# Outputs' loads and divisors moved to GpSimd, and the gated unit's first half put in source order on four engines

## The chip, the cores and the metric

The kernel runs on one core of a Trainium2 chip. The metric is the device time of one execution in microseconds (us). The kernel before takes 2924.66 us, the median of three runs (2924.26 to 2926.47). The engines are named as in the profile: PE is TensorE, DVE VectorE, ACT ScalarE, POOL GpSimd and SP SyncE; PEld is PE's weight load, and SPq, POOLq are the DMA-issuing sides of SP and POOL.

## The reference

One transformer layer whose two norms are modulated by a conditioning vector, with S = 2048 rows, D = 576, 32 heads of 18, and F = 4608, all in float32:

```
mod = silu(c) @ w_mod                      # six vectors of 576: sa, ca, ga, sb, cb, gb
h = layernorm(x) * (1 + ca) + sa
q, k, v = split(h @ wqkv)                  # 32 heads of 18
o = softmax(q @ k.T / sqrt(18)) @ v
x = x + ga * (o @ wo)
h = layernorm(x) * (1 + cb) + sb
x = x + gb * ((sigmoid(h @ w_gate) * (h @ w_up)) @ w_down)
```

## The kernel before

Every product is done in split form: an operand is cast to a high part (F32R), the difference to the original is the low part, and high x high, high x low and low x high are added.

The layer runs in three stages. Norm, q, k and v take the time up to about 237 us. Attention follows, to about 1580 us: 32 units (two heads and one half of the query rows each) of 16 steps; each step's PE work is written out by hand as a string of letters (`EASY`, `FULL`), and PE keeps that order (`manual_schedule`), while the other engines' instructions are put in order by the scheduler. Beside it run generators that advance by one `yield` at each letter "w", which is every second step, about 5 us. `taken` stores a unit's outputs (`od`) and sums of the softmax (`sd`). `divisors` loads the sums, takes the reciprocal, stores it (`rd`) and broadcasts it over each head's 18 rows into `rx`. `load_o` loads 128 rows' outputs, divisors and residual, and `project_o` multiplies them on POOL and projects them on PE (L667). Rows 0 to 7 (`first_rows`) go all the way to the operands of the gated unit; of rows 8 to 15 only the first heads are projected during attention (`last_rows_project`).

The gated unit follows. It has two halves of the rows; each half runs over 18 blocks of 256 columns of F, and each block has seven products in place of eight, in the order `ORDER = (1, 6, 2, 7, 5, 4, 3)`, with 14 matmuls each (`product`, L1029). After product 6 and product 7 stands one half of the previous block's product with w_down (`down`, L1052 to L1073: 48 matmuls in eight groups, three PSUM buffers `d`, and on DVE one add into `Oa` a group, L1069). In the first half the operands of the weights are made as well: `prepare(n + LOOK)` makes those of the product three places ahead. POOL makes sums of the raw weights (S, L884), ACT casts (w, L918), DVE takes the difference for the most of it and POOL for the rest (w, L923), and SP stores the result for the second half (ws, L924). What a product leaves is added on DVE from PSUM (u2 L1211, u3 L1222 and L1227, p1 L1234, u2 L1239), and `gate` (L1032 to L1045) follows: sigmoid on ACT, multiplication on DVE, cast hh on ACT, difference hl on DVE. The PSUM name `x` has three buffers in turn, so the add that reads the third step's product frees the buffer in which the next block's product 1 puts its second half.

Through the first half, `last_rows` (L1111 to L1185) advances by one `yield` at every second product: the divisors and projection of the last heads (80 matmuls, L1146), the layer norm of four rows at a time (statistics L153, scales L164 to L174, normalized rows L683, with `z` loaded back from `x1d` at L1163), its transposes and copies (ev, L1154), and the operands for the second half (ho, L714, with differences on POOL, L716, L721 and L725). From `n == ORDERED`, the 56th product (block 8), PE is held to source order; before that, and on all other engines throughout, the scheduler sets the order.

Of the kernel before, what the change touches and what calls it, by code (L numbers as in the profile page):

```python
# [15 lines left out]
F32 = mybir.dt.float32  # L16
# [7 lines left out]
P = 128  # L24
# [24 lines left out]
FULL = "vtmmttmvtm", "tmttwmtmm"  # L49
ORDERED = 56  # L50


@with_exitstack
def tile_block(ctx, tc, x_in, wqkv, wo, w_gate, w_up, w_down, c_in, w_mod, out):
# [181 lines left out]
    x1p = dram.tile([P, 8, D], F32, name="x1p")  # L236
    od = dram.tile([2, D, HW], F32, name="od")
    sd = dram.tile([2, H, HW], F32, name="sd")
    rd = dram.tile([2, H, HW], F32, name="rd")
    rx = dram.tile([2, D, HW], F32, name="rx")  # L240
    wod = dram.tile([P, 2, 2, D], F32R, name="wod")
# [383 lines left out]
    def load_o(t):  # L625

        half, a = divmod(t, 8)
        cols = slice(a * P, (a + 1) * P)
        n = 4 if half == 0 else DL // P
        got = state["rows", t % 2]  # L630
        for i, src in enumerate((od, rx)):
            nc.sync.dma_start(
                got[:, i, 0 : n * P].rearrange("p (k q) -> p k q", q=P),
                src[half, 0 : n * P, cols].rearrange("(k p) q -> p k q", p=P),
            )
            if half == 0:
                for p0 in (0, 64):
                    nc.sync.dma_start(got[p0 : p0 + 64, i, DM:640], src[half, DM:D, cols])
        nc.sync.dma_start(got[:, 2, 0:D], x_rows[:, t, :])

    def project_o(t):
# [3 lines left out]
        width = 640 if t < 8 else DL  # L645
        o, r, xt = got[:, 0, 0:width], got[:, 1, 0:width], got[:, 2, 0:D]
        T = temp([P, 2048], F32R)
# [95 lines left out]
    def first_rows():  # L743
        yield from load_wo()
        whole = big.tile([P, 8, 640], F32, name="big")
        for i in range(2):
            state["rows", i] = whole[:, 3 * i : 3 * i + 3, :]
        state["spare"] = whole[:, 6, :]
        yield from divisors(0, 0, H, state["spare"])
# [361 lines left out]
    def last_rows():  # L1111
# [5 lines left out]
        with tc.tile_pool(name="fin", bufs=1, side="right") as pool:  # L1117
            w = pool.tile([P, 2, 2, D], F32R, name="w")
            nc.gpsimd.dma_start(w, wod)
            yield from divisors(1, DL // DH + 1, H, pool.tile([P, 256], F32, name="sums"))  # L1120
            for t0 in (0, 4):
                cols = slice(t0 * P, (t0 + 4) * P)
                o, r = (pool.tile([P, 2, 512], F32, name=n) for n in ("o", "r"))
                for to, src in ((o, od), (r, rx)):
                    nc.sync.dma_start(to[:, 0, :], src[1, DL:DM, cols])
                    for p0 in (0, 64):
                        nc.sync.dma_start(to[p0 : p0 + 64, 1, :], src[1, DM:D, cols])
                yield
                nc.vector.tensor_mul(o, o, r)
                hi = pool.tile([P, 2, 512], F32R, name="hi")  # L1130
                nc.scalar.copy(hi, o)
                oh, om = hi[:, 0, :], hi[:, 1, :]
                ol = pool.tile([P, 512], F32R, name="ol")
# [3 lines left out]
                for j in range(4):  # L1137
                    rows = slice(j * P, (j + 1) * P)
                    xt = pool.tile([P, D], F32, name="xt", bufs=2)
                    nc.sync.dma_start(xt, x1p[:, t0 + j, :])  # L1140
                    for h in range(2):
# [3 lines left out]
                        for n, (a, i, k) in enumerate(ts_):  # L1145
                            nc.tensor.matmul(  # L1146
                                acc[:, :HALF], a[:, rows], w[:, i, k, cols], start=n == 0, stop=n == 4
                            )
                        nc.vector.tensor_add(xt[:, cols], xt[:, cols], acc[:, :HALF])
                    nc.sync.dma_start(x1d[:, t0 + j, :], xt)  # L1150
                    yield

        def modulated(ev, pt, scale, bias):
# [126 lines left out]
```

## Time and profile before

| | us |
|---|---|
| median of three runs | 2924.66 |
| the profiled execution, its time | 2923.8 |
| its span, first to last instruction | 2922.0 |
| gated unit, first half: blocks 0 to 17 | 1580.0 to 2273.3 |
| gated unit, second half, from | 2273.3 |
| PE busy | 2837.4 |
| DVE busy | 2127.2 |
| ACT busy | 1599.7 |
| POOL busy | 796.2 |

A row of the page's groups has line, engine and operation, out<-in with shapes, count, busy time, mean ns of one, and behind the bar the idle time of the engine just before them with what ended it. A row of waits has the engine and line, what it waited for, and then total, times and longest. A row of the timeline has start, length, engine, line and operation, with the idle time before it in brackets. The granted clock of PE is 1.00 at full speed.

### The profile page before, as it was taken

How to read it: one execution, taken by the hardware profiler on the slowest of the kernel's cores; microseconds unless marked ns; L12 is line 12 of the kernel's file. 1: busy time of each engine (PE TensorE's matmuls, PEld its weight loads, DVE VectorE, ACT ScalarE, POOL GpSimd, SP SyncE). 2: the span in 40 equal slices, each digit the busy share in tenths (PEclk: the TensorE clock that was granted, in tenths of full speed). 3: DMA queues.
4: the chain of work that ended last, by engine and by line, in shares of the span. 5: the costliest groups of instructions: out<-in, count | busy, mean ns of one | idle time of the engine just before them, and what ended most of it. 6: DMA issues, size and time to landing. Idle time of an engine off the chain costs nothing.

```text
span 2922.0 us, 46657 instructions
## 1 busy us (share of the span) xinstructions
PE 2837.4 (97%) x16933; PEld 1875.6 (64%) x16933; DVE 2127.2 (73%) x3865; ACT 1599.7 (55%) x2993; POOL 796.2 (27%) x894
## 2 busy tenths in 40 slices
PE   7999999999999999999999899998999999999999
PEld 5874444444444443443444788887888888888888
DVE  7567889999998888998771678765777555555555
ACT  3227999999998888899786323432333111111111
POOL 3102024444122101660222434456743100000000
PEclk9999999999999999999999999999999999999999
DMA  5344124433224211322326676776666844444443
GB/s 173 115 149 145 63 80 142 142 134 130 76 67 133 75 40 49 103 81 68 119 85 217 224 263 229 238 257 231 219 209 234 303 171 168 168 168 168 159 159 137
DMA packets 158204, 444.83 MB, mean 152 GB/s; under 512 B 19347, under 2 KB 71831, under 8 KB 145687
## 3 DMA queue, kind: packets, MB, share of 16 engines
q1 hardware_dynamic: 143495, 366.03, 37.5%
q0 software_dynamic: 14480, 75.84, 7.2%
q8 instruction: 133, 2.18, 0.3%
q14 instruction: 96, 0.79, 0.1%
HBM read 278.87 MB, written 167.12 MB: 153 GB/s over the span
## 4 chain that ended last, share of the span: by engine, by line
PE 87%; DMA 4%; DVE 3%; POOL 2%; issue 2%; ACT 1%; SPq 1%; POOLq 0%; ACTq 0%; DVEq 0%
PE o L543 17%; PE d L1065 14%; PE x L1029 13%; PE s L961 13%; PE s L451 11%; PE bg L1029 5%; PE bu L1029 5%; PE s L299 4%; PE s L339 2%; PE s L667 2%; DMA q<-qd 1%; DVE w L923 1%; ACT p L965 1%; DMA ws<-w 1%; POOL S L884 1%
## 5 line engine op out<-in xcount | busy, mean ns | idle before, releaser
L965 ACT ACTIVATE p<-s 128x512 f32<-128x512 f32 x2048 | 1063.4, 611 | 145.3 <-PE s L961 86.6
L464 DVE TENSOR_REDUCE mx<-s 128x1 f32<-128x512 f32 x1568 | 1010.7, 684 | 135.7 <-PE s L451 97.8
L451 PE MATMUL s<-k,q 54*128 54x512 f32 x1920 | 613.6, 443 | 3.9 <-DVE mx L464 2.3
L961 PE MATMUL s<-q,k 56*128 56x512 f32 x1920 | 594.0, 431 | 6.4 <-DMA q<-mrows 4.9
L543 PE MATMUL o<-p,vaug 128*32 128x512 f32 x4096 | 557.0, 610 | 1.0 <-ACT oT L558 1.0
L961 PEld LDWEIGHTS s<-q,k 56*128 56x128 f32 x1920 | 301.0, 187 | 321.1 <-ACT p L965 163.6
L1065 PE MATMUL d<-wd,hh 128*128 128x288 f32 x2304 | 471.4, 299 | 24.3 <-DVE Oa L1069 23.6
L451 PEld LDWEIGHTS s<-k,q 54*128 54x128 f32 x1920 | 290.3, 185 | 235.1 <-ACT p L965 105.7
L1065 PEld LDWEIGHTS d<-wd,hh 128*128 128x128 f32 x2304 | 379.7, 191 | 35.9 <-DVE Oa L1069 29.1
L1069 DVE TENSOR_TENSOR Oa<-Oa,d 128x288 f32<-128x288 f32 x576 | 257.3, 452 | 154.7 <-PE d L1065 151.5
L1065 PE MATMUL d<-wd,hl 128*128 128x288 f32 x1152 | 344.4, 299 | 0.9 <-DVE hl L1045 0.9
L1029 PE MATMUL x<-k,w 128*128 128x512 f32 x994 | 239.0, 391 | 3.7 <-DVE u L1239 2.6
L1041 ACT ACTIVATE u<-u 128x512 f32<-128x512 f32 x72 | 45.5, 632 | 328.4 <-DVE u L1227 306.6
L1065 PEld LDWEIGHTS d<-wd,hl 128*128 128x128 f32 x1152 | 220.2, 191 | 1.1 <-DVE hl L1045 1.1
L1029 PEld LDWEIGHTS x<-k,w 128*128 128x128 f32 x994 | 184.4, 188 | 41.7 <-DVE u L1239 3.5
L543 PEld LDWEIGHTS o<-p,vaug 128*32 128x32 f32 x4096 | 83.5, 109 | 165.4 <-issue 147.5
L1038 ACT ACTIVATE sg<-x 128x512 f32<-128x512 f32 x36 | 21.5, 598 | 292.4 <-PE x L1029 292.4
L1071 POOL DMA_DIRECT2D out_dram<-Oa x16 | 8.7, 542 | 606.6 <-DVE Oa L1069 606.6
L459 DVE CUSTOM_DVE_ANT_0 rise<-s,rise 128x512 f32<-128x512 f32 x240 | 163.3, 681 | 0.3 <-PE s L961 0.2
L457 ACT ACTIVATE rise<-s 128x512 f32<-128x512 f32 x240 | 147.8, 616 | 0.7 <-PE s L451 0.6
L923 POOL TENSOR_TENSOR w<-S,w 64x256 fp32r<-64x256 f32 x69 | 70.1, 1016 | 219.6 <-ACT w L918 208.3
L1029 PE MATMUL x<-w,w 128*128 128x512 f32 x504 | 122.1, 391 | 1.3 <-ACT w L918 1.0
(215 smaller groups left out, 3681.5 us busy)
## 6 DMA issues: line engine op xcount, KB each, us to landing
w<-ws SPq DMA_DIRECT2D x126, 640.0 KB
ws<-w SPq DMA_DIRECT2D x124, 640.0 KB
wd<-wds SPq DMA_DIRECT2D x36, 1152.0 KB
wds<-w POOLq DMA_DIRECT2D x18, 1152.0 KB, 4.6
k<-kd SPq DMA_DIRECT2D x30, 360.0 KB
w<-in_B_w_down_dram POOLq DMA_DIRECT2D x18, 576.0 KB, 4.3
q<-qd SPq DMA_DIRECT2D x64, 144.0 KB
raw<-in_B_w_gate_dram SPq DMA_DIRECT2D x34, 256.0 KB
```

What stands on the lines that cost most here:

```text
L299: nc.tensor.matmul(acc, w, hT[:, t, cols], start=n == 0, stop=n == len(ts_) - 1)
L451: nc.tensor.matmul(sp, qs[rows, qt * P : (qt + 1) * P], ks[rows, kc * 512 : (kc + 1) * 512], start=True, stop=True,)
L457: nc.scalar.activation(rise, sp, AF.Relu)
L459: nc.vector.tensor_tensor_reduce(rise, sp, rise, 1.0, -3.0e38, ALU.add, ALU.max, mx[0][:, qt, 0:1])
L464: nc.vector.tensor_reduce(mx[h][:, qt, j : j + 1], sp, axis=AX.X, op=ALU.max)
L543: nc.tensor.matmul(acc[32 * j : 32 * j + 32, :], vaug[:, kt, (2 * p + h) * VW : (2 * p + h) * VW + 32], probs[2 * c + h], start=kt == 0, s ...
L923: eng.tensor_sub(w[rows, :, to, :], src[rows, :, a, :], w[rows, :, a, :].bitcast(F32))
L961: nc.tensor.matmul(sT, ks[rows, kcols], qs[rows, c * 512 : (c + 1) * 512], start=True, stop=True)
L965: state["exp"] = nc.scalar.activation(pr, sT, AF.Exp, scale=SCALE)
L1029: nc.tensor.matmul(acc[v], w[:, v, a, :], X[s][:, b, :], start=first and n == 0, stop=n == 6, skip_group_check=not first,)
L1065: nc.tensor.matmul(acc[:, :HALF], a[:, f, rows], w[:, f, cols], start=n == 0, stop=n == 5)
L1069: nc.vector.tensor_add(Oa[:, t, cols], Oa[:, t, cols], acc[:, :HALF])
```

## The change

The diff has three parts. In the stores and loads of attention's outputs, `od` and `rx` become one tensor `orx`, a unit's four sums are stored by one DMA instead of four, and the loads of `load_o` and the three DMAs of `divisors` are issued by GpSimd instead of SyncE; the store of the reciprocals has a `yield` of its own between it and the reciprocal, and the residual rows have three tiles of their own. In `last_rows` the loads and stores go to GpSimd as well, a turn ahead or a turn later, and the multiplication, the copy and the differences are apart by `yield`s. In the main loop, PE, ACT, DVE and POOL are held to source order from product 0 to the end of the first half, and PE alone after it, where before PE alone was from product 56.

```
@@ taken
-            nc.sync.dma_start(od[half, f0 : f0 + DH, cols], oT[32 * j : 32 * j + DH, :])
-            nc.sync.dma_start(sd[half, 2 * p + h : 2 * p + h + 1, cols], oT[32 * j + DH : 32 * j + VW, :])
+            nc.sync.dma_start(orx[0, half, f0 : f0 + DH, cols], oT[32 * j : 32 * j + DH, :])
+        nc.sync.dma_start(
+            sd[half, 2 * p : 2 * p + 2, :].rearrange("h (c q) -> (h c) q", c=2), oT[DH:P:32, :]
+        )
@@ divisors
-        nc.sync.dma_start(t, flat(sd))
+        nc.gpsimd.dma_start(t, flat(sd))
         yield
         nc.vector.reciprocal(t, t)
-        nc.sync.dma_start(flat(rd), t)
-        yield
-        nc.sync.dma_start(
-            rx[half, h0 * DH : h1 * DH, :].rearrange("(h e) q -> h e q", e=DH),
+        yield
+        nc.gpsimd.dma_start(flat(rd), t)
+        yield
+        nc.gpsimd.dma_start(
+            orx[1, half, h0 * DH : h1 * DH, :].rearrange("(h e) q -> h e q", e=DH),
@@ load_o
-        got = state["rows", t % 2]
-        for i, src in enumerate((od, rx)):
-            nc.sync.dma_start(
+        got, xt = state["rows", t % 2], state["x", t % 3]
+        for i in range(2):
+            nc.gpsimd.dma_start(
                 got[:, i, 0 : n * P].rearrange("p (k q) -> p k q", q=P),
-                src[half, 0 : n * P, cols].rearrange("(k p) q -> p k q", p=P),
+                orx[i, half, 0 : n * P, cols].rearrange("(k p) q -> p k q", p=P),
             )
...
-        nc.sync.dma_start(got[:, 2, 0:D], x_rows[:, t, :])
+        nc.gpsimd.dma_start(xt, x_rows[:, t, :])
@@ last_rows
+            def load_heads_end(t0):
+                both = pool.tile([P, 2, 2, 512], F32, name="both")
...
+            def load_rows(j):
+                xt = pool.tile([P, D], F32, name="xt", bufs=3)
+                nc.gpsimd.dma_start(xt, x1p[:, j, :])
+                return xt
...
                 for j in range(4):
-                    nc.sync.dma_start(xt, x1p[:, t0 + j, :])
+                    if j < 3:
+                        rows.append(load_rows(t0 + j + 1))
+                    if j == 0 and t0 == 0:
+                        both = load_heads_end(4)
+                    if done:
+                        nc.gpsimd.dma_start(*done)
...
-                    nc.sync.dma_start(x1d[:, t0 + j, :], xt)
+                    done = x1d[:, t0 + j, :], xt
                     yield
@@ main loop
-        if n == ORDERED:
+        if n == 0:
+            manual.enter_context(tc.manual_schedule(engines={
+                mybir.EngineType.PE, mybir.EngineType.Activation, mybir.EngineType.DVE, mybir.EngineType.Pool,
+            }))
+        if n == 7 * NB:
+            manual.close()
             manual.enter_context(tc.manual_schedule(engines={mybir.EngineType.PE}))
```

Three places of the order, before and after. In the rows, the first number is the place on its engine, then the line, the operation, and the tiles; line numbers after the change are three higher for most of the gated unit.

DVE in the tail of a block of the first half, before; `u` is u3 at L1227 and u2 at L1239, `w` the low part of a weight:

```order
2648 L1227 TENSOR_TENSOR u_23237<-x,u_23237 128x512 x2
2649 L1042 TENSOR_TENSOR u_23237<-u_23237 128x512
2650 L923 TENSOR_TENSOR w<-S_23343,w 128x2x256
2651 L1234 TENSOR_TENSOR p_23089<-bg,p_23089 128x512
2652 L1045 TENSOR_TENSOR hl_23210<-u_23237,hh_23209 128x512
2653 L1234 TENSOR_TENSOR p_23089<-bu,p_23089 128x512
2654 L1042 TENSOR_TENSOR p_23089<-p_23089 128x512
2655 L923 TENSOR_TENSOR w<-raw_23068,w 128x2x256
2656 L1239 TENSOR_TENSOR u_23113<-x,u_23113 128x512
```

The same place after:

```order
2640 L926 TENSOR_TENSOR w<-raw_23201,w 128x2x256
2641 L1258 TENSOR_TENSOR u_23444<-x,u_23444 128x512 x2
2642 L1045 TENSOR_TENSOR u_23444<-u_23444 128x512
2643 L1048 TENSOR_TENSOR hl_23409<-u_23444,hh_23408 128x512
2644 L926 TENSOR_TENSOR w<-S_23550,w 128x2x256
2645 L1265 TENSOR_TENSOR p_23288<-bg,p_23288 128x512
2646 L1265 TENSOR_TENSOR p_23288<-bu,p_23288 128x512
2647 L1045 TENSOR_TENSOR p_23288<-p_23288 128x512
2648 L1048 TENSOR_TENSOR hl_23407<-p_23288,hh_23406 128x512
2649 L926 TENSOR_TENSOR w<-raw_23267,w 128x2x256
2650 L1270 TENSOR_TENSOR u_23320<-x,u_23320 128x512 x2
```

Each step's w has moved from behind the multiplication and between the next step's adds to ahead of the adds, and hl from among the next step's adds to the end of its own step.

DVE at the layer norm of four of the last rows, behind product 6, before; BN_STATS and BN_AGGR are the statistics, `z` the rows, `Oa` the adds of the down product:

```order
2674 L1069 TENSOR_TENSOR Oa<-Oa,d 128x288
2675 L154 BN_AGGR mv_2208<-st 128x2
2676 L1069 TENSOR_TENSOR Oa<-Oa,d 128x288
2677 L164 TENSOR_SCALAR var<-mv_2208 128x4
2678 L1069 TENSOR_TENSOR Oa<-Oa,d 128x288
2679 L923 TENSOR_TENSOR w<-raw_23068,w 128x2x256
2680 L1069 TENSOR_TENSOR Oa<-Oa,d 128x288 x2
2681 L169 RECIPROCAL r_23474<-sd 128x4
2682 L171 TENSOR_TENSOR sd<-r_23474 128x4
2683 L1069 TENSOR_TENSOR Oa<-Oa,d 128x288
2684 L172 TENSOR_TENSOR sd<-sd,var 128x4
```

The same place after:

```order
2662 L153 BN_AGGR mv_2207<-st 128x2
2663 L152 BN_STATS st<-z 128x6 x2
2664 L153 BN_AGGR mv_2207<-st 128x2
2665 L163 TENSOR_SCALAR var<-mv_2207 128x4
2666 L168 RECIPROCAL r_23705<-sd 128x4
2667 L170 TENSOR_TENSOR sd<-r_23705 128x4
2668 L171 TENSOR_TENSOR sd<-sd,var 128x4
2669 L172 TENSOR_SCALAR sd<-sd 128x4
2670 L173 TENSOR_TENSOR rs_2208<-r_23705,sd 128x4
2671 L684 TENSOR_SCALAR z<-z,mv_2207,rs_2208 128x2x288 x4
2672 L1072 TENSOR_TENSOR Oa<-Oa,d 128x288 x8
```

The adds into Oa, which stood among the norm's instructions, now all stand behind the last of them.

GpSimd in attention, after, at the divisors of the second half's first heads; these DMAs were on SyncE before:

```order
351 L631 DMA big<-orx 128x3x128 x2
352 L572 DMA big<-sd 88x256
353 L576 DMA rd<-big 88x256
354 L578 DMA orx<-rd 396x1x1024
355 L631 DMA big<-orx 128x3x128 x2
356 L650 TENSOR_TENSOR big<-big 128x384
```

All of them now stand in one queue, with the multiplication that needs the loads right behind them. The loads of `z` stay on SyncE; after, their place there is:

```order
604 L864 DMA raw_22801<-in_B_w_up_dram 128x1x256
605 L927 DMA ws<-w 128x1280 x2
606 L1189 DMA z<-x1d 128x288 x8
607 L927 DMA ws<-w 128x1280
608 L862 DMA raw_23267<-in_B_w_gate_dram 128x2x256
```

The eight loads stand behind two stores of weight pairs.

More of the change, by code (lines that the diff above doesn't have):

```diff
@@ L49 @@
 FULL = "vtmmttmvtm", "tmttwmtmm"
-ORDERED = 56
 @with_exitstack
@@ L746, in first_rows @@
         for i in range(2):
-            state["rows", i] = whole[:, 3 * i : 3 * i + 3, :]
-        state["spare"] = whole[:, 6, :]
+            state["rows", i] = whole[:, 2 * i : 2 * i + 2, :]
+        for i in range(3):
+            state["x", i] = whole[:, 4 + i, 0:D]
+        state["spare"] = whole[:, 7, :]
         yield from divisors(0, 0, H, state["spare"])
@@ L1146, in last_rows @@
                             nc.tensor.matmul(
-                                acc[:, :HALF], a[:, rows], w[:, i, k, cols], start=n == 0, stop=n == 4
+                                acc[:, :HALF], a[:, part], w[:, i, k, cols], start=n == 0, stop=n == 4
                             )
                         nc.vector.tensor_add(xt[:, cols], xt[:, cols], acc[:, :HALF])
-                    nc.sync.dma_start(x1d[:, t0 + j, :], xt)
+                    done = x1d[:, t0 + j, :], xt
                     yield
+            nc.gpsimd.dma_start(*done)
         def modulated(ev, pt, scale, bias):
```

40 lines of the change are left out of this document (24 added, 16 removed).

## The prediction

> **What bounds the kernel now.** I read the page first, then a table of windows cut at the gated unit's block borders, then PE's waits there, then the timelines of one undisturbed block.
>
> ```profile
> span 2922.0 us, 46657 instructions
> PE 2837.4 (97%) x16933; PEld 1875.6 (64%) x16933; DVE 2127.2 (73%) x3865; ACT 1599.7 (55%) x2993; POOL 796.2 (27%) x894
> ```
>
> TensorE (PE) is busy for 97% of the span, so the work itself stays and only PE's waits, and the half clock behind a long wait, can go or come. They are found by block. In the rows below (stretch, its length, then PE, PEld, DVE, ACT, POOL busy with counts, and PE's granted clock) each stretch is one block of the first half, from block 0; the row of 693.30 is the whole half.
>
> ```profile
> 1580.00:1605.40 25.40, 23.09 (x99) 18.14 (x98) 11.66 (x17) 10.26 (x15) 9.57 (x10) 1.00 0.80 269
> 1605.40:1647.40 42.00, 38.43 (x195) 32.17 (x196) 33.18 (x47) 13.69 (x21) 26.30 (x24) 0.96 0.79 269
> 1647.40:1696.30 48.90, 43.12 (x225) 37.31 (x224) 31.10 (x51) 13.12 (x20) 14.86 (x16) 0.93 0.54 181
> ...
> 1776.20:1814.50 38.30, 36.57 (x207) 32.13 (x206) 32.07 (x64) 15.49 (x22) 18.17 (x19) 1.00 0.73 242
> 1814.50:1851.20 36.70, 36.70 (x209) 32.44 (x208) 26.37 (x41) 14.06 (x21) 16.98 (x15) 1.00 0.67 232
> ...
> 1925.70:1966.90 41.20, 37.27 (x195) 32.39 (x194) 27.55 (x42) 15.10 (x24) 30.52 (x26) 0.96 0.80 277
> ...
> 2055.10:2098.40 43.30, 37.77 (x195) 33.31 (x194) 30.36 (x44) 13.86 (x22) 31.71 (x28) 0.92 0.62 218
> ...
> 2168.30:2203.30 35.00, 35.00 (x195) 31.12 (x195) 25.68 (x42) 11.42 (x18) 16.88 (x16) 1.00 0.62 211
> ...
> 1580.00:2273.30 693.30, 654.55 (x3525) 573.11 (x3525) 489.91 (x784) 232.23 (x346) 347.27 (x317) 0.98 0.70 238
> ```
>
> Block 15 (from 2168.30) has no wait: 35.0 us. Were all like it, the half would take 23.1 (PE's work in block 0) + 17 x 35.0 = 618.1 us. It takes 693.3, so 75.2 us are excess: 9.3 in blocks 0 and 1, 13.9 in block 2, 32.7 in blocks 9 to 12 (1925.7 to 2098.4 is 172.7, less 140.0), the other 19.3 in the blocks between. This 75.2 is all that a better order can win; PE's waits of this stretch, and ACT's idle time ahead of its copies of the last rows' operands, say who ends them:
>
> ```profile
> PE d L1065 <- DVE Oa L1069: 23.6, 12, 4.7
> PE x L1029 <- DVE u L1239: 2.6, 2, 1.4
> L714 ACT CAST ho<-B 128x512 fp32r<-128x512 f32 x21 | 13.0, 621 | 50.7 <-DMA xs<-ho 27.5 <-DMA B<-hs 15.7 <-POOL B L725 6.2
> ```
>
> PE waits above all for DVE's adds into Oa, which free the three banks of the down product; and ACT stood 27.5 us behind copies whose buffer was still being stored, with the gate's own steps queued behind.
>
> **The change part by part.** I count after's excess in the same way, in five terms, from the rows of before.
>
> First, the tail of a block (products 5, 4, 3). This is block 15 from 2195 us, DVE and then ACT (start, length):
>
> ```profile
> 2197.99 0.69 DVE L1042 TENSOR_TENSOR u<-u 128x512 f32<-128x512 f32 x1
> 2198.60 1.24 DVE L923 TENSOR_TENSOR w<-S,w 128x512 fp32r<-128x512 f32 x1
> 2199.76 0.68 DVE L1234 TENSOR_TENSOR p<-bg,p 128x512 f32<-128x512 f32 x1
> ...
> 2202.25 0.72 DVE L1042 TENSOR_TENSOR p<-p 128x512 f32<-128x512 f32 x1
> 2202.89 1.23 DVE L923 TENSOR_TENSOR w<-raw,w 128x512 fp32r<-128x512 f32 x1
> 2204.04 0.68 DVE L1239 TENSOR_TENSOR u<-x,u 128x512 f32<-128x512 f32 x1
> ```
>
> ```profile
> 2198.72 0.62 ACT L1044 CAST hh<-u 128x512 fp32r<-128x512 f32 x1 [0.56 <-DVE u L1042]
> ...
> 2200.47 0.63 ACT L1041 ACTIVATE p<-p 128x512 f32<-128x512 f32 x1 [1.13 <-DVE p L1234]
> 2201.01 0.82 ACT L918 CAST w<-raw 128x768 fp32r<-128x768 f32 x1
> ```
>
> The add at 2204.04 frees the bank that the next block's product 1 needs for its second half. It ends at 2204.72 and PE does not wait, so the need is at 2204.72 or a little later. The scheduler had put each weight pair's cast and difference (w) behind the gate's multiplication, where they hide. In source order both come first in each step: on ACT the next cast stands behind this step's hh, on DVE w stands ahead of the adds. From the end of hh at 2199.34: cast 0.82, w 0.69 or 1.23, add 0.68, sigmoid 0.63, multiply 0.72, hh 0.62, then cast 0.82, w 0.69 or 1.23, add 0.68: the bank comes free at 2199.34 + 6.35 to 7.43 = 2205.7 to 2206.8, which is 1.0 to 2.1 us late. Engines overlap neighbouring instructions by some 0.08, so the low end is about 0.65; against the second, the Oa adds a little late as well, 2.3 is the high end. The two lengths of w come from these rows, in which one cast releases DVE's and GpSimd's (POOL's) part together:
>
> ```profile
> 2185.39 0.69 DVE L923 TENSOR_TENSOR w<-S,w 128x512 fp32r<-128x512 f32 x1 [0.15 <-ACT w L918]
> 2185.43 1.24 POOL L923 TENSOR_TENSOR w<-S,w 64x256 fp32r<-64x256 f32 x1 [5.63 <-ACT w L918]
> ...
> 2198.24 1.05 POOL L923 TENSOR_TENSOR w<-S,w 64x256 fp32r<-64x256 f32 x1 [8.02 <-ACT w L918]
> ```
>
> DVE, first by 0.04, took 0.69 and POOL 1.24; in the pair before 2199 POOL was first by 0.36 and took 1.05, DVE 1.24. The Trainium skill, "SBUF — State Buffer", section "Who interferes with whom", says the same as a rule: of a DVE instruction with two SBUF inputs and a GpSimd one that reads SBUF, the first to start has the shared port for its whole length. By that rule the late bank is a matter of who starts first: 1.0 us per block if DVE always does, 2.1 if never. In source order both parts are ready at the cast's end with nothing ahead, as at 2185.39, so I take 1.2 a block, near the low end; 16 blocks make 19 us (10 to 37).
>
> Second, the layer norm of the last rows (8 BN_STATS, 4 aggregates, the scales, 4 norms, for four rows at a time, twice). In before it was spread among the Oa adds (the first of the two):
>
> ```profile
> 1780.08 2.92 SPq L1163 DMA_DIRECT2D z<-x1d  x5
> 1786.42 0.46 DVE L153 BATCH_NORM_STATS2 st<-z 128x6 f32<-128x288 f32 x1 [0.53 <-DMA z<-x1d]
> 1791.78 2.10 DVE L683 TENSOR_SCALAR z<-z,mv,rs 128x576 f32<-128x576 f32 x4
> ```
>
> and the group of those adds:
>
> ```profile
> L1069 DVE TENSOR_TENSOR Oa<-Oa,d 128x288 f32<-128x288 f32 x576 | 257.3, 452 | 154.7 <-PE d L1065 151.5
> ```
>
> Its block, from 1776.20, paid 38.30 - 36.57 = 1.7 us. The order of after has all of it, to the last norm, ahead of the eight Oa adds of the down product's first half, twice, in a step of product 6. A product takes 3.2 to 3.3 (block 0: 23.09 for seven), so the two halves of down take 12 to 12.6 of block 15's 35.0: 6.3 each, 48 matmuls of 0.13 in eight groups of 0.8. Counted from a block's start, products 1 and 6 are done at 6.4, and down needs its first bank back three groups on, at 8.8. The loads of z stand on SP behind the store of a weight pair that the same step's POOL part ends, about 6 on; eight issues (2.92 for 5) take 4.7, the last lands some 3.4 after its issue (1783.0 to 1786.42), so at 14 to 15.5; the rest of the norm, last statistics to last scaled row without the Oa adds between, takes 4.3 to 4.5 (7.46 in the rows, 1786.42 to 1793.88, less the seven Oa adds that the order puts among it, 0.45 each: 4.3). End: 18.5 to 20, 10 to 11 after the need; with loads that get out sooner, 7. Behind such a wait PE runs slow:
>
> ```profile
> 1991.74 0.53 PE L1065 MATMUL d<-wd,hh 128*128 128x288 f32 x2 [3.18 <-DVE Oa L1069]
> 1993.64 0.85 PE L1065 MATMUL d<-wd,hh 128*128 128x288 f32 x2 [0.84 <-DVE Oa L1069]
> 1994.52 0.68 PE L1065 MATMUL d<-wd,hh 128*128 128x288 f32 x2
> 1999.56 2.78 PE L1029 MATMUL x<-k,w 128*128 128x512 f32 x11
> ```
>
> From 1993.64 to 1999.56 one matmul took 0.24 (0.88 + 0.72 x 7 for 24) where 0.133 is usual: 24 of them, 2.6 us lost. The Trainium skill, "TensorE: Matmul & The Clock Gate", section "What's actually happening", gives an idle window of about 3.4 us before the clock halves, and as long until it recovers; the 3.18 here already did it with the 0.84 behind it, so the trace is a little harsher, and by the page a stall of 10 would lose 1.7 instead of 2.6. I take 10 + 2.5, twice: 25 us (16 to 30).
>
> Third, the last rows' own PE work, which is in both: 80 matmuls and 48 transposes. Block 6 is 1.7 us longer than block 15 for 14 more, 0.12 each: 15 us.
>
> Fourth, their work on ACT and POOL between the gate's steps (21 ho copies of 0.62, 12 ev, 40 POOL differences by the code). Every second step has a turn, so 3 in 7 fall in the tail: 14 of 33 ACT pieces at 0.7 (0.62 and the row below) are 10 us, and 17 of 40 POOL pieces, each making one DVE instruction 0.55 longer (1.24 - 0.69), 9.4: 20 us. If ACT's waits for B stay too, half of 15.7 is on top (28); if the turns fall kindly, 8. The new loads and stores on POOL, 0.5 us of issue each, lie in this: a load that waits for the broadcast holds the next weight parts, which are made three products ahead (10 us), and that is the cover; without it the wait would be PE's.
>
> ```profile
> L1154 ACT ACTIVATE ev<-d,mcol 128x512 f32<-128x512 f32 x12 | 9.3, 773 | 0.0
> ```
>
> Fifth, blocks 0 and 1: in source order ACT and DVE wait for the first loads and for POOL's sums in their turn, where before had other work ready. Between the 9.3 of before and 20, I take 9.3 plus one pair and one difference of sums (these rows), 14.
>
> ```profile
> 2173.00 2.78 POOL L884 TENSOR_TENSOR S<-raw 128x384 f32<-128x384 f32 x2 [0.68 <-DVE w L923]
> 2176.67 2.31 POOL L884 TENSOR_TENSOR S<-raw,raw 128x384 f32<-128x384 f32 x2
> ```
>
> Sum: 19 + 25 + 15 + 20 + 14 = 93 against 75.2: +18.
>
> In attention the change takes a wait away. The divisors of the second half's first heads, as the chain tells it, then PE's waits, and the window:
>
> ```profile
> 1385.11 9.84 DMA rx<-rd
> PE s L667 <- POOL t L652: 4.0, 1, 4.0
> 1387.00:1460.00 73.00, 68.75 (x441) 31.27 (x440) 55.32 (x106) 54.88 (x109) 15.14 (x19) 0.94 0.39 122
> ```
>
> The broadcast of the divisors took 9.84 us, and the projection's matmuls, whose place in PE's order is fixed by hand, came 4.0 too early. One more turn (5.2 us) between reciprocal and store moves them back by more than that, and the half clock goes with it: in the 73 us of that window PE lost 4.25. I take -6 (-9 to 0; 0 if GpSimd's queue, with the loads behind one another, is that much slower). The single store of sd and the loads on GpSimd cost nothing else there: POOL is busy 15.14 of 73.
>
> So 2923.8 (the profiled execution, 1.8 over its span) + 18 - 6 = 2936 us; the median of the runs is 0.9 above that execution.
>
> **The rivals.**
>
> Faster: source order ends the waits that the scheduler's order made. For it: the 32.7 us of blocks 9 to 12 and 13.9 of block 2 come with Oa adds and ho copies issued in a bad order, and later blocks show that 35.0 can be had. It decides at the add of the tail, and at the norm: if the bank comes free within what PE allows after 2204.72 (ACT's cast would have to be done before hh ends) and z lands before product 6 is over, the terms are tail 0, norm 6, own work 15, inserts 10, start 9.3: 40, so -35 - 6: 2883 us. Against it: the tail's sum leaves 0.65 even at its best.
>
> No change: tail at its low end 10, norm 20, own work 15, inserts 20, start 9.3, and nothing won in attention: 74 for 75, about 2924.
>
> Slower by far: POOL is first at the port in nearly every step. Tail 2.1 x 16 = 34, norm 30, the rest as forecast: 113, 2923.8 + 38 - 6 = 2956. For it: in the tail of block 15 DVE was second both times (1.24, 1.23). The port rule of the page named above allows this as well as the forecast; one row with DVE first is thin.
>
> **How the numbers follow.** 0.2% is 5.8 us, about what a measurement can tell: no change is 2919 to 2930. Chances: forecast 0.45 (its own range 2912 to 2950, of which some 0.03 lies under 2919 and 0.03 inside no change), faster rival 0.31, no change 0.14, far slower 0.10. So faster 0.34, same 0.17, slower 0.49. The range has to take in most of the faster rival and of the slow one: 2886 to 2958.
>
> **What would show it.** In the profile after: PE waits for DVE's u2 adds about once a block, 0.7 to 2 us, and blocks 14 to 17 take 36 to 37 us instead of 35.0; two waits of d for Oa of 7 us or more, each right behind a layer norm on DVE, and half-speed matmuls behind them; no wait of the projection's matmuls for POOL at 1395 to 1399; ACT's waits for xs<-ho gone. If blocks stay at 35.0 and the two norms cost under 3 us each, I am wrong and the faster rival holds.

## The result and the profile after

The change makes the kernel slower: 2999.23 us median of four runs (2997.72 to 2999.77) against 2924.46 us before in the same session, a ratio of 1.0266 with a 95% interval of 1.0253 to 1.0279. The direction was forecast, the size was not: 75 us in place of 12, and outside the range.

The page's head, for the profiled execution after:

```profile
span 2997.1 us, 46472 instructions
PE 2851.1 (95%) x16933; PEld 1889.1 (63%) x16933; DVE 2089.0 (70%) x3865; ACT 1597.8 (53%) x2993; POOL 846.9 (28%) x989
```

PE has the same 16,933 instructions and is busy 13.7 us longer, which goes with a lower granted clock (in the gated unit's first half 0.93 in the mean, 0.98 before); the rest of the 75.1 us of span is waiting. The gated unit starts at 1571.8 in place of 1580.0, its second half at 2348.7 in place of 2273.3. So attention and what is ahead of it won 8.2 us and the first half lost 83.6. These are windows cut at block borders again: blocks 0, 1, 2, 6, 8, then 9 to 12 and 13 to 16 together, block 15 alone, and the whole half.

```profile
1571.80:1601.10 29.30, 25.41 (x99) 20.44 (x99) 11.30 (x16) 10.67 (x15) 15.51 (x14) 0.88 0.71 258
1601.10:1642.80 41.70, 37.80 (x195) 32.93 (x194) 27.97 (x46) 12.66 (x20) 19.86 (x20) 0.92 0.74 256
1642.80:1686.50 43.70, 38.16 (x196) 33.68 (x194) 26.01 (x42) 12.27 (x19) 18.39 (x19) 0.92 0.65 200
1812.40:1866.20 53.80, 37.88 (x205) 33.62 (x204) 30.71 (x64) 14.35 (x21) 17.41 (x21) 0.84 0.52 175
1904.30:1957.00 52.70, 39.37 (x206) 34.71 (x205) 30.81 (x64) 15.67 (x24) 17.93 (x19) 0.84 0.52 175
1957.00:2128.60 171.60, 152.20 (x793) 132.87 (x792) 95.18 (x164) 52.18 (x81) 84.47 (x76) 0.94 0.64 220
2128.60:2311.40 182.80, 150.51 (x778) 130.95 (x777) 96.21 (x165) 52.09 (x81) 94.15 (x84) 0.93 0.53 186
2215.50:2261.70 46.20, 38.94 (x196) 33.79 (x195) 21.87 (x38) 12.00 (x19) 22.90 (x20) 0.93 0.47 167
1571.80:2348.70 776.90, 673.59 (x3526) 588.83 (x3526) 450.83 (x783) 229.50 (x345) 353.92 (x344) 0.93 0.61 212
```

Blocks 6 and 8, with the two layer norms, take 53.8 and 52.7 us; block 15, which took 35.0 before, takes 46.2, with PE busy 38.9 of it at a clock of 0.93. In excess over 618.1 us, the half has 158.8 (93 were forecast): 12.9 in blocks 0 and 1, 72.3 in blocks 2 to 9, 71.3 in blocks 10 to 16, 2.3 in block 17. Against the kernel before, the loss stands in few places. Blocks 9 to 12 take about as long as before (171.6 us, 172.7 before), and block 2 is shorter (43.7, 48.9 before). Blocks 6 and 8 are 33.1 us longer together (36.7 each before), and blocks 13 to 16 take 182.8 us where they took 139.9. Before, ScalarE's copies of the last rows' operands (ho) ran from 1932 to 2069 us and were over by block 12; in source order they go on from 2012 to 2273, through block 16.

PE's waits in this half, whole list:

```profile
PE d L1068 <- DVE Oa L1072: 59.6, 16, 15.9
PE x L1032 <- DVE u L1270: 39.6, 15, 7.9
PE x L1032 <- ACT p L1236: 3.9, 1, 3.9
```

It waits for VectorE in two places, the adds into Oa and the u2 adds of the tail, the two that the prediction named. But VectorE is busy less than before (450.8 us of the half, 489.9 before). What VectorE waits for, and then ScalarE, is the line that matters most:

```profile
DVE w L926 <- ACT w L921: 140.7, 49, 50.4
...
DVE hl L1048 <- ACT hh L1047: 49.7, 71, 0.7
...
DVE st L152 <- DMA z<-x1d: 14.5, 3, 8.6
```

```profile
ACT w L921 <- POOL S L887: 58.3, 23, 6.7
```

Apart from one wait of 50.4 at the unit's start, VectorE stood 90 us for ScalarE's casts of weights (before: 23.4), and ScalarE stood 58.3 us for GpSimd's sums (before: 18.7). One such chain, in the tail of block 11, first ScalarE, then GpSimd, then VectorE:

```profile
2078.72 0.62 ACT L1047 CAST hh<-u 128x512 fp32r<-128x512 f32 x1 [1.81 <-PE bg L1032]
2079.25 0.61 ACT L715 CAST ho<-B 128x512 fp32r<-128x512 f32 x1
2085.19 0.83 ACT L921 CAST w<-S 128x768 fp32r<-128x768 f32 x1 [5.33 <-POOL S L887]
```

```profile
2079.99 1.28 POOL L717 TENSOR_TENSOR ho<-B,ho 128x512 fp32r<-128x512 f32 x1 [13.30 <-issue]
2081.24 1.98 POOL L887 TENSOR_TENSOR S<-raw,raw 128x384 f32<-128x384 f32 x2
2083.17 1.99 POOL L887 TENSOR_TENSOR S<-S,raw 128x384 f32<-128x384 f32 x2
```

```profile
2079.38 0.69 DVE L1048 TENSOR_TENSOR hl<-u,hh 128x512 fp32r<-128x512 f32 x1 [0.74 <-ACT hh L1047]
2086.05 0.69 DVE L926 TENSOR_TENSOR w<-S,w 128x512 fp32r<-128x512 f32 x1 [5.98 <-ACT w L921]
2086.66 0.68 DVE L1265 TENSOR_TENSOR p<-bg,p 128x512 f32<-128x512 f32 x1
```

GpSimd had been idle for 13.30 us ahead of its ho difference, though the sums S behind it needed nothing but raw weights. The profile names nothing that ended this wait ("issue"); the rows show it: ho starts at 2079.99, as ScalarE's ho copy ends (2079.25 + 0.61), and that copy stands behind hh, which waited for the gate. Only then come the two pairs of sums (4 us), the cast, w, and behind w the add of p at 2086.66, some 8 us after the product that it reads was done. That is one full round through three engines that each hold their order, and PE gets the tail's bank late:

```profile
2091.50 2.08 PE L1032 MATMUL x<-k,w 128*128 128x512 f32 x4 [6.46 <-DVE u L1270]
```

### The profile page after: what moved, and what is told of

It reads as the page before. It is cut to its first block, busy times and chain, and to the rows that moved or that the text cites. A ratio compares the mean times of both kernels' runs of the same rounds, so it can differ in the third digit from the quotient of the medians.

```text
span 2997.1 us, 46472 instructions
## 1 busy us (share of the span) xinstructions
PE 2851.1 (95%) x16933; PEld 1889.1 (63%) x16933; DVE 2089.0 (70%) x3865; ACT 1597.8 (53%) x2993; POOL 846.9 (28%) x989
## 4 chain that ended last, share of the span: by engine, by line
PE 78%; issue 6%; DVE 5%; DMA 4%; POOL 3%; ACT 3%; SPq 1%; POOLq 0%; ACTq 0%; DVEq 0%
PE o L541 16%; PE d L1068 13%; PE s L964 12%; PE x L1032 11%; PE s L449 10%; PE bg L1032 4%; PE bu L1032 4%; PE s L297 3%; PE s L337 2%; POOL S L887 2%; PE s L668 2%; ACT w L921 1%; DVE w L926 1%; POOL w L926 1%; DVE mx L462 1%
## 5 line engine op out<-in xcount | busy, mean ns | idle before, releaser
L1032 PE MATMUL x<-k,w 128*128 128x512 f32 x994 | 251.3, 403 | 39.6 <-DVE u L1270 39.6
L926 POOL TENSOR_TENSOR w<-S,w 64x256 fp32r<-64x256 f32 x69 | 80.6, 1169 | 208.7 <-ACT w L921 184.7
```

Source lines behind the costliest of these rows:

```text
L926: eng.tensor_sub(w[rows, :, to, :], src[rows, :, a, :], w[rows, :, a, :].bitcast(F32))
L1032: nc.tensor.matmul(acc[v], w[:, v, a, :], X[s][:, b, :], start=first and n == 0, stop=n == 6, skip_group_check=not first,)
```

## The experiments

Four explanations stood against one another: the order of the three engines beside PE; PE's own order from block 0; the loads and stores in GpSimd's queue; and, within the order, which place of it. Times are medians; "before" was 2921.6 to 2924.2 in the sets of runs. In the code cuts, names of engines and some subscripts are shortened.

### The two parts of the change alone

The first kernel has all of the change but the order:

```
-        if n == 0:
-            manual.enter_context(tc.manual_schedule(engines={PE, Activation, DVE, Pool}))
-        if n == 7 * NB:
-            manual.close()
+        if n == 56:
             manual.enter_context(tc.manual_schedule(engines={mybir.EngineType.PE}))
```

> All of the change but the order: loads, divisors and stores on GpSimd, while only TensorE is held to source order, from product 56 as before. Order theory (the first half's loss comes from holding VectorE, ScalarE and GpSimd to source order): attention keeps its 8 us gain, the first half stays near the 693 us of before, total about 2916 us (2906 to 2926). Queue theory (the loads and stores in GpSimd's queue make the loss): first half above 735 us, total above 2960 us.

Measured: 2916.65 us, ratio 0.9981 (0.9969 to 0.9994). The unit starts at 1573.5, and its first half takes 695.0 us. This is what the order theory has: the loads and stores on GpSimd are a small gain, not the loss.

The second has the kernel before with the order of the change, the same lines put in the other way round.

> The kernel before with only the main loop's order of the change (four engines in source order through the first half); loads, divisors and stores on SyncE as before. Order theory: attention as before, first half 755 to 785 us in place of 777, total 2985 to 3010 us. Queue theory: first half under 720 us, total under 2950 us.

Measured: 3017.52 us, 1.0325 (1.0308 to 1.0342); attention ends at 1580.5 as before. The first half takes 789.7; it and the total are a little above their ranges. The order carries the loss. The half is 13 us longer here than in the change (776.9), about the size of one wait that the change does not have; ahead of it VectorE stood 11.3 us for a load of residual rows (xt), which the change issues earlier:

```profile
PE d L1065 <- DVE Oa L1069: 63.2, 14, 14.5
PE x L1029 <- DVE u L1244: 35.9, 15, 7.9
PE d L1065 <- DVE xt L1149: 12.7, 1, 12.7
```

The third holds PE alone to source order, but from product 0:

```
-            manual.enter_context(tc.manual_schedule(engines={PE, Activation, DVE, Pool}))
+            manual.enter_context(tc.manual_schedule(engines={PE}))
```

> The changed kernel with TensorE alone held to source order from product 0 on; VectorE, ScalarE and GpSimd by the scheduler. If the loss lies in the other three engines' order: about 2917 us as with the loads and stores alone (2907 to 2930). If TensorE's own order of the first eight blocks has a part in it: above 2940 us.

Measured: 2915.81 us, 0.9978 (0.9965 to 0.9991). PE's order from block 0 costs nothing. This and the first are the versions that beat both kernels, by 0.2%; they cannot be told apart.

### Which place in the order

The layer norm behind the eight Oa adds:

```
-        if n >= 5 and n % 2:
-            next(rows2, None)
         if before is not None and k in (6, 7):
             down(before, k - 6)
+        if n >= 5 and n % 2:
+            next(rows2, None)
```

> The changed kernel with one call moved: the last rows' turn stands behind the down product's half of its step, so that the layer norm stands behind the eight Oa adds on VectorE. If the norm ahead of the Oa adds costs 16 us each time: the two waits of 15.9 and 13.1 us go or fall under 5, total 2970 us (2960 to 2980). If the wait is for the reload of z and would only show elsewhere: blocks 6 and 8 stay above 45 us, total above 2990 us.

Measured: 2986.43 us, 1.0222 (1.0207 to 1.0237): 13 us won, less than the first expectation had. Blocks 6 and 8 still take 48.1 us each, as the second had it. The waits there are 10.61 and 6.57, now for the Oa adds of the next half of down: behind the norm, VectorE's order has more adds that PE needs, and these come late instead.

The reload of z a turn ahead of the statistics:

```
                     for g in range(2):
                         nc.sync.dma_start(z[:, g, 0:HALF], x1d[...])
-                    ln_stats(zp, x1, mv2[:, t, :])
                     zs.append(z)
+                yield
+                for t, z in zip(range(4 * ch, 4 * ch + 4), zs):
+                    ln_stats(zp, z[:, :, 0:HALF], mv2[:, t, :])
```

> The changed kernel with the reload of z issued one turn (two products) ahead of the layer norm's first statistics. Reload theory (VectorE stands 9.1 and 5.4 us for z, behind a store of x1d issued on GpSimd in the same turn): the waits of 15.9 and 13.1 us fall to about 7 each, total 2984 us (2978 to 2990). If the norm's own length on VectorE makes the wait: under 4 us won, total above 2994 us.

Measured: 2972.29 us, 1.017 (1.015 to 1.019): 27 us won, more than the 15 expected. VectorE no longer waits for z, and block 6 takes 43.6, block 8 36.1. The extra turn also moved the norm to another product: the second now stands ahead of a u2 add, which lets PE wait 7.87 us at the start of block 9.

GpSimd's sums one product earlier, ahead of the last rows' turn:

```
         prepare(n + LOOK)
+        sums(n + LOOK + 1)
         st = block(n)
```

with the lines that make S1, S2 and S3 moved from the function of the weights into `sums`.

> The changed kernel with GpSimd's sums of the raw weights (S) issued one product earlier, so that they stand ahead of the last rows' differences (ho) of the turn before, and not behind them. Chain theory (in blocks 10 to 16 GpSimd's ho stands ahead of S, ScalarE's cast waits for S, VectorE's w for the cast, and the adds behind w wait with it): the u2 waits of 6.5 to 7.9 us fall below 3, the Oa waits of 3 to 5 us there go, total about 2967 us (2955 to 2980). Theory of plain work (the last rows' pieces on ScalarE and GpSimd cost what they last, wherever they stand): under 8 us won, total above 2990 us.

Measured: 2959.25 us, 1.0123 (1.0101 to 1.0145): 40 us won, as the chain theory had it. ScalarE's and then PE's waits in the half:

```profile
ACT w L931 <- POOL S L887: 13.5, 13, 4.7
```

```profile
PE d L1078 <- DVE Oa L1082: 43.5, 7, 16.4
PE x L1042 <- DVE u L1287: 24.6, 15, 4.6
PE x L1042 <- ACT p L1253: 3.9, 1, 3.9
```

ScalarE's wait for S has fallen from 58.3 to 13.5, the u2 waits from 39.6 to 24.6, and blocks 10 to 16 take 37 to 44 us. What is left in d are mostly the two norms (16.4 and 13.2). The copies ho still go on to 2232 us, into block 16, so their later place alone is not the loss: blocks 10 to 16 have 30 us of excess here and 71 in the change.

Both together:

> The changed kernel with both: GpSimd's sums one product earlier (won 40 us alone) and z reloaded one turn ahead (won 27 us alone). If the two losses are separate places of the order: they add, total 2932 us (2926 to 2938). If one hides the other: above 2945 us.

Measured: 2931.24 us, 1.003 (1.0017 to 1.0042): the two add up, 68 us where 67 had been won one by one. They are separate losses, and together they are 68 of the 75 us.

### Where the weights stand: two misses

> The changed kernel with one call moved: the weights three products ahead are prepared behind the gate's step, not ahead of it, so that on ScalarE and VectorE the cast and the difference of a weight stand behind the adds and the gate. If the tail's loss (39.6 us of waits for the u2 adds, and most waits of blocks 10 to 16) is the weights standing ahead of the adds: blocks 14 to 16 fall from 45 to 50 us to 37 or less, total about 2945 us (2930 to 2960), and the two layer norms stay at 16 us each. If the last rows' work itself is the loss: blocks 10 to 16 lose under 3 us each, total above 2980 us.

```
-        prepare(n + LOOK)
         st = block(n)
...
+        prepare(n + LOOK)
         if n >= 5 and n % 2:
             next(rows2, None)
```

Measured: 3103.67 us, 1.0625 (1.0605 to 1.0646): 104 us worse than the change, the other way than expected. In a repeated sequence, w behind one step's gate is w ahead of the next step's adds: the edit did not take the weights from ahead of the adds, it only shifted which product they belong to and started the sums later. ScalarE's and VectorE's waits in the half:

```profile
ACT w L921 <- POOL S L887: 162.1, 52, 5.6
```

```profile
DVE w L926 <- ACT w L921: 212.7, 53, 50.5
```

> The changed kernel with the weights of a step that has a gate prepared between the gate's multiplication and its copy hh, so that the cast runs on ScalarE between sigmoid and hh and w on VectorE between the multiplication and hl, as the scheduler had placed them. Tail theory (w ahead of the adds makes the u2 adds late by 1 to 3 us a block): the u2 waits of blocks 1 to 9 (0.5 to 2.9 us each) go below 0.3, total 2975 us (2960 to 2985). If the length of the chain is the same in this order: same time as the change, 2999 us.

```
         (sigmoid, multiplication)
+        weights()          # prepare(n + LOOK)
         nc.scalar.copy(st["hh", r][:, f, :], t)
```

Measured: 3056.84 us, 1.0457 (1.0433 to 1.0481), outside both expectations. Here the cast that waits for S stands ahead of hh as well (ScalarE waits 122.0 for S). With the sums and z ahead the same place was tried again:

> As the kernel with sums and z ahead, and the weights prepared between the gate's multiplication and hh as well. If that place was bad alone (57 us lost) only since the late sums then held hh: with the sums early the tail's waits (24.6 us for the u2 adds) go, total 2915 us or less. If the place itself is bad, w standing on VectorE ahead of hl and the Oa adds: above 2945 us.

Measured: 3017.02 us, 1.0314 (1.0294 to 1.0334), against 2931.24 without it. The place itself is bad. VectorE's groups in this kernel, and then in the one without the edit (e9):

```profile
L936 DVE TENSOR_TENSOR w<-raw,w 128x512 fp32r<-128x512 f32 x55 | 65.9, 1198 | 53.3 <-ACT w L931 52.9
...
L1059 DVE TENSOR_TENSOR hl<-u,hh 128x512 fp32r<-128x512 f32 x35 | 46.9, 1339 | 0.7 <-ACT hh L1058 0.7
```

```profile
L936 DVE TENSOR_TENSOR w<-raw,w 128x512 fp32r<-128x512 f32 x55 | 41.7, 759 | 57.4 <-ACT w L931 56.9
...
L1058 DVE TENSOR_TENSOR hl<-u,hh 128x512 fp32r<-128x512 f32 x35 | 25.6, 732 | 25.0 <-ACT hh L1057 25.0
```

The sums now run on GpSimd while VectorE does w, hl and the multiplication, which read two operands from SBUF: this w takes 1.20 us instead of 0.76, hl 1.34 instead of 0.73, and the multiplication 0.97 instead of 0.82. In e9 the sums mostly lay beside adds that read PSUM, and those keep their length in both kernels (Oa 0.45, the adds of p 0.68). So the edit put a w and an hl that are 1.6 and 1.8 times as long into the very chain that it was meant to shorten.

### Which engine's order

The set of engines of the change, less one or two:

> The changed kernel with VectorE left to the scheduler and TensorE, ScalarE and GpSimd held to source order through the first half. If the loss comes through VectorE's order (w ahead of the adds, the norm ahead of the Oa adds): 2930 us or less. If it comes from ScalarE's and GpSimd's order (cast behind late sums, ho ahead of sums): above 2965 us.

> The changed kernel with GpSimd left to the scheduler; TensorE, VectorE and ScalarE held to source order through the first half. If GpSimd's order (ho ahead of the sums) makes the waits of blocks 10 to 16, as the 40 us of the earlier sums say: about 2960 us (2950 to 2970), with both norms still at 16 us or so. If the sums are late whoever orders GpSimd, since ScalarE's copies ho come late: above 2985 us.

> The changed kernel with ScalarE left to the scheduler; TensorE, VectorE and GpSimd held to source order. If the cast standing behind hh and ho on ScalarE is a large part: 2965 us or less. If VectorE's and GpSimd's order alone carry the loss: above 2985 us.

> The changed kernel with TensorE and VectorE held to source order, ScalarE and GpSimd by the scheduler. VectorE's order alone then costs what the norms (29 us of waits) and the tail (12 us in blocks 1 to 9, 1 to 2 a block after) take: 2955 us (2945 to 2970). If VectorE's order only hurts together with late casts: 2930 us or less.

```
-            manual.enter_context(tc.manual_schedule(engines={PE, Activation, DVE, Pool}))
+            manual.enter_context(tc.manual_schedule(engines={PE, Activation, Pool}))   # e12
+            manual.enter_context(tc.manual_schedule(engines={PE, Activation, DVE}))    # e13
+            manual.enter_context(tc.manual_schedule(engines={PE, DVE, Pool}))          # e14
+            manual.enter_context(tc.manual_schedule(engines={PE, DVE}))                # e15
```

| left to the scheduler | us | ratio to before (95%) |
|---|---|---|
| none (the change) | 2999.23 | 1.0266 (1.0253 to 1.0279) |
| VectorE | 2969.80 | 1.0159 (1.0138 to 1.0179) |
| ScalarE | 2948.74 | 1.0083 (1.0064 to 1.0102) |
| GpSimd | 2935.99 | 1.0042 (1.0024 to 1.006) |
| ScalarE and GpSimd | 2950.52 | 1.0093 (1.0061 to 1.0124) |
| all three (e8) | 2915.81 | 0.9978 (0.9965 to 0.9991) |

The gains (29, 50, 63) are more together than the 83 of all three: the loss is a round through three engines, and each of them that may go ahead takes something out of it. GpSimd takes out most; that this is for its idle time, and because its sums need nothing but loads, is argued and not shown. Free engines do not simply add either: ScalarE and GpSimd free are 15 us slower than GpSimd alone, and why was not followed. PE's waits with GpSimd free:

```profile
PE d L1068 <- DVE Oa L1072: 28.2, 11, 11.6
PE x L1032 <- DVE u L1268: 28.0, 15, 7.1
```

The longest u2 wait, 7.1, is at the start of block 1. Of the others, six are 0.5 to 1.0 us and five about 1.8, these five where a copy ho stands in the tail of the block ahead; two of 2.5 have `ol` and `hi` there, one of 2.7 an ho as well; the waits of 11.62 and 10.35 are the norms. GpSimd free was expected at 2950 to 2970 and came out better (5 of its 63 us are an earlier start of the unit, at 1566.6); ScalarE free agrees with a large part for the cast's place. VectorE free came out above 2965, as its second expectation had it for a loss through ScalarE's and GpSimd's order: there ScalarE still waits 71.3 us for S, PE no longer waits for u2 at all, and its waits for Oa are 67.0. With the other two free, VectorE's order alone costs 35 us (2950.5 against 2915.8), as expected.

Two tries to take away the rest with GpSimd free, z a turn ahead, and then the norm behind down as well:

> GpSimd left to the scheduler (2936 us alone) and z reloaded a turn ahead. The two norms still cost 11.6 and 10.4 us of waits with GpSimd free, of which VectorE stood 3.5 and 2.5 for z. If the norm's loss is separate from GpSimd's order: both waits fall to 5 to 7, total 2923 us (2916 to 2930). If the earlier reload displaces other loads on SyncE: no gain, 2936 us or more.

> As the kernel before it, with the last rows' turn behind the down product's half as well, so that the norm stands behind the Oa adds on VectorE. If the norm's length ahead of the Oa adds is what is left there: the waits of blocks 6 and 8 go, total 2908 to 2918 us, below the 2916 us of TensorE held alone if the tail's 2 us a block were all that is left. If it only moves to the next adds behind: as the kernel before it, within 5 us.

Measured: 2928.98 us, 1.0027 (1.0015 to 1.004), and 2932.81 us, 1.0032 (1.002 to 1.0045). The first agrees with its first expectation, though only one of the two waits fell to 6.7: the other is 8.45, now for a u2 add at the start of block 9. In the second PE's waits for Oa go nearly to nothing (1.4 us in all), but its u2 waits rise from 35.2 to 42.5, and the half takes 707.9 us after 707.1. Not all of that rise is the norm: the first norm moves on to the adds behind it (1.1 and 1.7 us), the second still costs 8.45, and a new wait of 7.1 at the start of block 11 comes from ScalarE's ho copy, which stood 5.33 us for a load of B with a weight's cast behind it. No order by hand on VectorE tried here reaches the scheduler's. Sums and z ahead for the scheduler gave nothing either:

> TensorE alone held to source order from product 0, the other three by the scheduler (2915.8 us), with sums and z ahead. If the scheduler takes the earlier places: the Oa waits of blocks 9 to 13 (some 25 us there) shrink, total 2895 to 2908 us. If it sets its own order whatever the source has: 2911 to 2920 us.

Measured: 2934.41 us, 1.0038 (1.0024 to 1.0052), 19 us worse than without them and outside both expectations: blocks 11 to 14 take 43.7 to 48.7. The scheduler does take other places from another source order, and not better ones. Why these are worse was not followed further.

## Why the prediction was wrong

**The inserts** (the fourth term, 20 us for the last rows' pieces on ScalarE and GpSimd) are the step that failed. The sum priced each piece by its own length (0.7 on ScalarE, 0.55 of lengthening on VectorE for one on GpSimd) and not by what waits behind it, and it counted on a lead: "the next weight parts, which are made three products ahead (10 us), and that is the cover". The weights are three products ahead of PE, and PE indeed hardly waits for a weight. But VectorE has no such lead: w stands in its order ahead of the adds of the present step, so a w that could be 10 us late for PE is late at once for the add behind it. Taking away the late sums won 40 us alone. The waits of ScalarE for S also follow the time over four kernels with the same work and the same engines in source order: 13.5 us at 2959, 58.3 at 2999, 122.0 at 3057, 162.1 at 3104.

**The tail** has the right mechanism, and its 19 us are near the u2 waits without late sums (18.8 us) only by luck. With no piece of the last rows in it, the tail came out at the low end of the sum: 6.2 us from the end of hh to the end of the add (6.35 in the sum), and PE waited 0.53 where 1.2 was taken:

```profile
1645.09 1.89 PE L1032 MATMUL x<-k,w 128*128 128x512 f32 x7 [0.53 <-DVE u L1270]
```

Two borders of blocks have this 0.53; two more, with the projection's matmuls beside them, have no wait. The other u2 waits are inserts again: 20.8 us in three waits behind late sums (6.46, 6.46 and 7.87), 2.0 each behind a copy ho, 2.93 each where VectorE's own pieces for the projection (`ol` and `hi`, which the prediction did not price) stand ahead of w, 0.2 to 0.7 with a copy `ev`, and 3.9 at the start of block 1. That VectorE would mostly be first at the port held: w takes 0.73 to 0.75 in the mean after (1.03 to 1.07 before).

**The norm** was right in its place and too small: 10 us of wait and 2.5 of half clock each were forecast; the waits were 15.9 and 13.1, and blocks 6 and 8 were 18.8 and 17.7 us over, with some of the last rows' own work in them. The term at fault is the time of z's loads, "about 6 on". In the run they went out 14.1 after block 6 began, on SyncE, behind a store that GpSimd issued in the same turn (GpSimd, then SyncE, then what SyncE's queue waited for):

```profile
1818.32 1.25 POOL L926 TENSOR_TENSOR w<-S,w 64x256 fp32r<-64x256 f32 x1 [0.96 <-ACT w L921]
1819.51 0.56 POOL L1177 DMA_DIRECT2D x1d<-xt  x1
```

```profile
1817.97 1.96 SPq L927 DMA_DIRECT2D ws<-w  x2
1826.54 3.64 SPq L1189 DMA_DIRECT2D z<-x1d  x8
```

```profile
SPq L1189 <- DMA x1d<-xt: 6.3, 1, 6.3
```

SyncE was done with the weights' stores at 1819.9 and then stood 6.6 us, 6.3 of it for the store of x1d to land, which took 6.7 us from its issue. The diff shows the store, delayed by a turn; the prediction counted the queue that z stands in, not what z reads. Block 8 has no such store ahead of z: three of its loads of z went out at 1904.3, the other five at 1913.5, behind loads and stores of weights on SyncE. With the store a turn earlier and on SyncE (the order alone) VectorE still stood 15.8 us for z, so neither GpSimd's queue nor that turn is the whole reason. What the runs show is that statistics in the turn of the reload wait for it, and a turn later do not.

**The start** came out as taken: blocks 0 and 1 have 12.9 us of excess, 14 were forecast. The last rows' own work on PE (15 us) is the same in both kernels and was not measured by itself.

**Attention** won 8.2 us, 6 were forecast, but not by the step named. The wait of the projection's matmuls is still there, as long as before:

```profile
PE s L668 <- POOL t L653: 4.0, 1, 4.0
PE s L668 <- POOL t L654: 0.9, 1, 0.9
```

The chain of waits has the broadcast, and behind it a load that also takes its time:

```profile
1380.40 10.00 DMA orx<-rd
1390.39 0.28 issue
1390.67 6.38 DMA big<-orx
```

The broadcast was over at 1390.4, 4.6 us earlier than before, and the load behind it took 6.4: the extra turn was used up by that load. Of the 8.2 us, some 2 stand before attention begins and the others come in small pieces. The 17 kernels with the change's loads and stores start the gated unit at 1566.6 to 1576.5 us, the two without them at 1580.0 and 1580.5, so they bring 3.5 us or more; which of them does it was not tried. Differences of 5 us between totals can come from this start alone.

**The rivals**: the faster one asked that the source order end the waits for Oa in blocks 2 and 9 to 12. Block 2 did become shorter (43.7 us for 48.9); in blocks 9 to 12 PE's waits for Oa fell from about 20 us to 10, and u2 waits of 9 took their place. The far slower one had the direction, but by the port, which lengthened only few of VectorE's instructions in the change (a w of 1.37 us, an hl of 1.40); it acted in e10, at a place that was not in the prediction. Of the signs that the prediction named, the two long waits behind the norms came, and ScalarE's waits for xs<-ho went; the projection's wait stayed, and blocks 14 to 16 took 45 to 50 us in place of 36 to 37.

## What to carry to other kernels

When several engines are put in source order together, follow one round through them: an instruction that has slack for its reader has none for what stands behind it on its own engine. In a fixed order, put work that needs only loads (here the sums, one product earlier) ahead of work that waits for the round, and a reload a turn ahead of its use; the same source gave a worse order when the scheduler set it. Moving a block of work from one end of a step to the other does not take it out of the round; check where it stands among the instructions of the round, and what runs beside it.

## What the runs showed of the hardware that was not expected

GpSimd's sums beside VectorE's instructions with two SBUF operands are the larger case of the 0.69 and 1.24 of the prediction. These rows are from the kernel with sums and z ahead and the weights inside the gate (e10):

```profile
2081.55 1.51 DVE L936 TENSOR_TENSOR w<-raw,w 128x512 fp32r<-128x512 f32 x1
2082.98 1.50 DVE L1059 TENSOR_TENSOR hl<-sg,hh 128x512 fp32r<-128x512 f32 x1
```

```profile
2081.49 2.44 POOL L887 TENSOR_TENSOR S<-raw,S 128x384 f32<-128x384 f32 x2
```

In the mean over e10 an hl of u took 1.34 us (0.73 without the edit); the single w and hl here took 1.5 beside a pair of sums of 2.44 (1.98 elsewhere). The Trainium skill, "SBUF — State Buffer", section "Who interferes with whom", has the second to start blocked for the first's whole length. Here both sides were longer, VectorE's instructions by 0.6 to 0.8 and a pair of sums by 0.5, which would fit engines that take turns by instruction; that was not tried by itself.

PE's clock halved behind shorter waits than the 3.18 us of the prediction: after one wait of 2.93 us, with no other within 30 us, the granted clock was 0.50 from 1690.7 to 1694.1 and 1.00 on both sides of it.
